# Expert units that leave y in PSUM over their end, loop conversions a step earlier, eight w_out tiles ahead

## The chip, the cores and the metric

The kernel runs on one core of a Trainium2 chip. The metric is the device time of one execution in microseconds (us), the median of several runs. Before the change it was 1417.6 us, the median of three runs from 1417.41 to 1417.85.

## The reference

All inputs but two are float32; `moe2_w_in` and `moe2_w_out` are float64.

```python
# attention: q, k, v are (8, 8, 576, 64); keys and values are averaged in blocks of 8
k_p, v_p = k.reshape(B, H, 72, 8, D).mean(3), v.reshape(B, H, 72, 8, D).mean(3)
scores = q @ k_p.T / sqrt(D)
attn = exp(scores - max); attn /= attn.sum(-1) + 1e-9
x = (attn @ v_p) as (4608, 512)
# first MoE: each of 4608 tokens goes to one of 8 experts (512 -> 1024 -> 512)
logits = x @ w_gate + modality_bias[modality_id]
e = argmax(logits); gate = softmax(logits)[e]
x = gate * (relu(x @ w1[e]) @ w2[e])
# second part, all tokens (512 -> 2048 -> 512)
h = x @ w_in
out = (h * clip(h + 3, 0, 6) / 6) @ w_out
```

## The kernel before

Float32 products are made of three matmuls of the type fp32r: each operand is split into a part hi, rounded to that type, and a rest lo, and hi·hi, hi·lo and lo·hi are summed in PSUM. A split costs a copy on ACT (hi, L771) and a subtraction on DVE (lo, L772).

The program has three stages. **Attention** and routing (to some 200 us) scatter the tokens to DRAM (`xr`), sorted by expert. The **units** (`moe1`, from some 197 to 648 us) each take 400 rows of one expert; this input makes twelve. Unit 0 is written out (`first`), eight run in a hardware loop (`For_i`, L1030), two follow in fixed code (`fs=0`, `fs=1`) and one is `last`. **`moe2`** (648 us to the end) computes the dense layers in 6 blocks of 768 tokens by 8 quads each; a quad has seven products `mm` (Strassen's scheme in Winograd's form) and twelve groups `o_group` of the product with `w_out`, which the next quad runs among its own `mm`.

A unit has eight steps f = 0..7, one for each 128 of the 1024 hidden columns. In step f, `h_mm(f)` makes 12 matmuls into a `ph` bank, ACT and DVE make hi and lo of its relu (L926, L927), and `y_mm(f - 1)` adds 12 matmuls into the four banks y0 to y3 (L935). `w_dma` loads the weights three steps ahead into two buffers `ws` (L865, L867), and `w_split` splits them two steps ahead on ACT and DVE. The next unit's rows (`cxg`) are loaded in steps 1 to 4, multiplied by their gate on POOL, and transposed on TensorE at the unit's end: `transp(c)` makes four transposes (L856; for c = 0 a fifth, L858, for the token numbers), and `split` takes them out of one of two `pt` banks as `xhi`, `xlo`. So `transp(2)` needs the bank of `transp(0)`, whose last reader is the copy `tkr` on ACT (L861), and `transp(3)` that of `transp(1)`, whose last reader is DVE's `xlo`.

At a unit's end PE runs `h_mm(7)`, `transp(0)`, `transp(1)`, `y_mm(6)`, `transp(2)`, `transp(3)`, `y_mm(7)`; then DVE copies y0 and y2 to `yo`, and ACT y1 and y3 (L1024), and `store_y` sends `yo` to DRAM in step 3 of the next unit.

While it runs, each unit of the loop also converts two pieces of the float64 `w_in` into the seven combinations that the quads use (`conv`, 13 operations each: 2 on ACT, 11 on DVE, loaded by L889, stored by L909). The fixed units and the first quads convert tiles of `w_out` (`wo_conv`, 9 operations each: 2 on ACT, 7 on DVE). `EARLY` names the tiles that are converted before `moe2`, `REST` those in its first block, where the list `cops` holds the operations and `extra[i]` places them behind product i of a quad.

PE, ACT, DVE and SP run what the program writes, in that order; an engine that waits holds back all that is behind it. All loads and most stores are issued by SP, so a store whose data are not ready also holds back the loads behind it. The loop's end is a branch on each engine; when the loop is left, all engines meet at a barrier.

Of the kernel before, what the change touches and what calls it, by code (L numbers as in the profile page):

```python
# [8 lines left out]
F32 = mybir.dt.float32  # L9
# [10 lines left out]
P = 128  # L20
# [9 lines left out]
NW = 400  # L30
# [8 lines left out]
YB = 8  # L39
NP = NT // (2 * TB)  # L40
NQ = F2 // (2 * P)
EARLY = (0, 8, 1, 9, 2, 10)
REST = (3, 11, 4, 12, 5, 13, 6, 14, 7, 15)
ORDER = (0, 4, 1, 5, 3, 2, 6)
KR = (0, 160, 288, 448)
GROUPS = ((0, 5), (5, 5), (10, 5), (15, 5), (20, 5), (25, 5), (30, 3), (33, 2), (35, 1))
# [752 lines left out]
def moe1(tc, g, xr_d, tok_d, y_d, s_d, w1, w2, w_in):  # L799
# [4 lines left out]
    def pool(n, b, st=es_l, **kw):  # L804
        return st.enter_context(tc.tile_pool(name=n, bufs=b, reuse_waits="tile", **kw))
# [18 lines left out]
    def open_ps():  # L824
        s.psy = pool("psy", 1, es_p, space=PSUM)
        s.psh = pool("psh", 2, es_p, space=PSUM)
        s.pst = pool("pst", 2, es_p, space=PSUM)

    def open3():
        g.open_w()  # L830
# [49 lines left out]
        gate_x()  # L880
        return i_

    def store_y(col):
        return nc.sync.dma_start(y_d.rearrange("(d p) n -> p d n", p=P)[:, :, bass.ds(col, NW)], s.yo)

    def conv_load(c, h, half):
        t = s.cs[h]
# [22 lines left out]

    def unit(i, first=False, last=False, tail=None, quad=None, fs=None):
        e = s.e0 if first else reg(0, i, E - 1)
        yps = [s.psy.tile([P, NW], F32, name=f"y{d}", tag=f"y{d}") for d in range(4)]
        hh = {}

        def h_mm(f):
            j = f % 4
            n = 0
            ph = s.psh.tile([P, NW], F32, name="ph", tag="ph")
            for k in range(4):  # L920
                for a, b in ((s.wh, s.xhi), (s.wh, s.xlo), (s.wl, s.xhi)):
                    nc.tensor.matmul(ph, a[j][:, 0, k * P:(k + 1) * P], b[k], start=(n == 0), stop=(n == 11))  # L922
                    n += 1
            hi = s.hp.tile([P, NW], F32R, name="hi", tag="hi")
            lo = s.hp.tile([P, NW], F32R, name="lo", tag="lo")
            nc.scalar.activation(hi, ph, AF.Relu)  # L926
            nc.vector.scalar_tensor_tensor(lo, ph, 0.0, hi.bitcast(F32), op0=ALU.max, op1=ALU.subtract)  # L927
            hh[f] = (hi, lo)

        def y_mm(f):  # L930
            j = f % 4
            hi, lo = hh.pop(f)
            for d in range(4):
                for n, (a, b) in enumerate(((s.wh, hi), (s.wl, hi), (s.wh, lo))):
                    nc.tensor.matmul(yps[d], a[j][:, 1, d * P:(d + 1) * P], b, start=(f == 0 and n == 0), stop=(f == 7 and n == 2))  # L935

        lx = LX if first else 1
        parts = {LX: (0, 1, 2, 3)} if first else {1: (0,), 2: (1,), 3: (2,), 4: (3,)}
        ops = []
        for f in range(8):  # L940
            if first and f == 0:
                w_dma(e, 2)
            if f == lx and not last:
                en = reg(0, i + 1, E - 1)
            if f < 5 or not last:
                w_dma(e if f < 5 else en, (f + 3) % 8)
            if f == 0 and not first:
                col = reg(5, i, NT)
                if quad is not None:
                    cc, cn = (nc.values_load(g.tab[0:1, 6, bass.ds(quad + d, 1)], engines=(ET.SP,), min_val=0, max_val=NQ - 1) for d in range(2))  # L950
            if f < 6 or not last:
                w_split((f + 2) % 8)
            h_mm(f)
            if f in parts and not last:
                load_x(i + 1, parts[f])
            if f - 1 in parts and not last:
                gate_x(parts[f - 1])
            if f == 2:
                store_tok(NT if first else reg(5, i + 1, NT))
            if f == 3 and not first:  # L960
                store_y(col)
            if f == 7 and not last:
                for c in range(2):
                    transp(c, ps())
            if f > 0:
                y_mm(f - 1)
            if tail and next(tail, None):
                open3()
            if first and f in (5, 6):
                conv_load(0, 0, f - 5)  # L970
            if first and f in (6, 7):
                g.wo_load(EARLY[f - 6])
            if first and f == 6:
                s.n_l = nc.values_load(g.nun, min_val=NQ, max_val=NQ + 8)
            if last:
                if f in (1, 2):
                    g.y_load(0, f - 1)
                if f == 3:
                    ops = g.y_ops(0)
                if f == 3:  # L980
                    nc.sync.dma_start(g.tk, tok_d[NW:NW + NT].rearrange("(c p) -> c p", p=P))
                if f == 7:
                    pt = ps()
                    nc.tensor.transpose(pt[:, 0:NT // P], g.tk, g.idn[0:NT // P, 0:NT // P])
                    nc.vector.tensor_copy(g.tki, pt[:, 0:NT // P])
                if f >= 1:
                    g.s_load()
                if f >= 3:
                    for _ in range(3):
                        if ops:  # L990
                            ops.pop(0)()
                if f >= 6:
                    g.wo_load(REST[f - 6])
            elif quad is not None:
                if f == 1:
                    co, ops = conv(s.cs[0])
                if f == 4:
                    c1_, ops = conv(s.cs[1])
                for _ in range(5):
                    if ops:  # L1000
                        ops.pop(0)()
                if f == 4:
                    conv_store(co, cc, 0)
                if f in (0, 1):
                    conv_load(cc, 1, f)
                if f in (5, 6):
                    conv_load(cn, 0, f - 5)
                if f == 7:
                    conv_store(c1_, cc, 1)
            elif fs is not None:  # L1010
                if f in (0, 2, 4):
                    ops += g.wo_conv(EARLY[3 * fs + f // 2])
                for _ in range(4):
                    if ops:
                        ops.pop(0)()
                n = 3 * fs + f // 2 + 1
                if f in (2, 4, 6) and n < len(EARLY):
                    g.wo_load(EARLY[n])
        if not last:
            for c in range(2, 4):  # L1020
                transp(c, ps())
        y_mm(7)
        for d in range(4):
            (nc.scalar.copy if d % 2 else nc.vector.tensor_copy)(s.yo[:, d], yps[d])  # L1024

    def run(tail):
        open_ps()
# [18 lines left out]
def moe2(tc, g, out):  # L1046
# [131 lines left out]
    yo = []  # L1178
    for j in range(NP):
        for q in range(NQ):  # L1180
            extra = {i: [] for i in range(7)}
            if j == 0:
                for i in range(7):
                    for _ in range(2):
                        if cops:
                            extra[i].append(cops.pop(0))
            if j + 1 < NP:
# [136 lines left out]
```

## Time and profile before

| | |
|---|---|
| median of 3 runs | 1417.6 us |
| profiled execution, its own time | 1416.87 us |
| its span, first to last instruction | 1415.1 us |
| granted TensorE clock, mean | 0.992 of full speed |
| busy: PE, DVE, ACT, POOL | 97%, 67%, 44%, 11% |

The profiled execution is 0.7 us faster than the median, and its time is 1.8 us longer than its span. Busy time of PE is no measure of its rate, since its matmuls overlap: one is shown with 340 ns and more, and the next one starts some 180 ns after it. What a wait costs is read from the distance of the starts. In a timeline, the bracket behind an instruction is the idle time before it and what ended it. The stage of the units is read at places where PE's order is the same in all units: their ends.

### The profile page before, as it was taken

The page shows a single profiled execution, that of the slowest core. Times are in us where ns is not written, and L with a number is a line of the kernel's source. Part 1 is how long each engine was busy: PE and PEld are TensorE (multiplying, and loading weights), DVE is VectorE, ACT ScalarE, POOL GpSimd, SP SyncE. Part 2 cuts the span into 40 slices and gives each one's busy share as a digit, 9 for nine tenths or more (in the row PEclk, how much of TensorE's full clock was granted, in tenths as well). Part 3 has the DMA queues.
Part 4 walks back from the last instruction along what each step waited for, and adds up shares of the span by engine and source line. Part 5 has one row for each costly group of instructions (what it writes and reads, how often), then busy time and mean ns, then how long its engine had stood idle before and what let it go on. Part 6 is the DMA issues. An engine that isn't in the chain of part 4 may idle for free.

```text
span 1415.1 us, 24118 instructions
## 1 busy us (share of the span) xinstructions
PE 1368.4 (97%) x7594; PEld 1263.5 (89%) x7594; DVE 947.2 (67%) x1929; ACT 627.6 (44%) x1276; POOL 159.3 (11%) x191
## 2 busy tenths in 40 slices
PE   7998989999999999999999999999999999999997
PEld 5888878999999999998888889888988888888886
DVE  6999785788888887876777445645644564465443
ACT  3576664555555554553444333423432343243322
POOL 3132331111111111100000100100010010001001
PEclk8899999999999999999999999999999999999999
DMA  9996356777777776675653544554354455345441
GB/s 254 314 273 203 108 167 197 245 245 246 246 244 243 243 241 199 188 223 169 202 163 114 184 142 120 159 162 119 120 181 140 120 150 173 116 119 164 115 116 67
DMA packets 229781, 254.40 MB, mean 180 GB/s; under 512 B 19256, under 2 KB 191836, under 8 KB 229692
## 3 DMA queue, kind: packets, MB, share of 16 engines
q1 hardware_dynamic: 223932, 233.16, 54.7%
q0 software_dynamic: 5760, 20.10, 4.0%
q8 instruction: 50, 0.82, 0.3%
q14 instruction: 39, 0.32, 0.1%
HBM read 206.74 MB, written 46.47 MB: 179 GB/s over the span
## 4 chain that ended last, share of the span: by engine, by line
issue 56%; PE 3%; POOL 2%; DVE 1%; ACT 0%; POOLq 0%; DVEq 0%; ACTq 0%
POOL out_dram L1074 2%; PE ph L922 2%; PE y L935 1%; DVE wl L772 0%; DVE wo L795 0%; DVE lo L927 0%; PE pt L856 0%; POOLq L1319 0%; ACT wh L771 0%; ACT dex L780 0%; DVE dex L794 0%; DVE dm L785 0%; DVE da L783 0%; ACT hi L926 0%; POOLq L1074 0%
## 5 line engine op out<-in xcount | busy, mean ns | idle before, releaser
L1095 PE MATMUL hps<-yc,sq 128*128 128x384 f32 x2004 | 405.2, 337 | 3.0 <-ACT s L1136 1.2
L1095 PEld LDWEIGHTS hps<-yc,sq 128*128 128x128 f32 x2004 | 358.2, 188 | 37.1 <-ACT s L1136 5.4
L1085 PE MATMUL ops<-wo,gh 128*128 128x512 f32 x1152 | 358.4, 392 | 0.0
L1085 PEld LDWEIGHTS ops<-wo,gh 128*128 128x128 f32 x1152 | 211.4, 188 | 23.1
L1085 PE MATMUL ops<-wo,gl 128*128 128x512 f32 x576 | 228.7, 397 | 0.0
L1107 ACT ACTIVATE r<-c,three 128x384 f32<-128x384 f32 x144 | 88.9, 617 | 207.8 <-DVE c L1117 205.8
L772 DVE TENSOR_TENSOR wl<-ws,wh 128x512 fp32r<-128x512 f32 x192 | 137.8, 751 | 33.4 <-ACT wh L771 29.3
L1111 ACT CAST gh<-r 128x384 fp32r<-128x384 f32 x192 | 98.6, 514 | 129.5 <-DVE r L1108 128.1
L771 ACT CAST wh<-ws 128x512 fp32r<-128x512 f32 x192 | 114.4, 619 | 76.0 <-DMA ws<-in_moe_w_dram 58.2
L922 PE MATMUL ph<-xhi,wh 128*128 128x400 f32 x384 | 132.3, 345 | 3.5 <-issue 1.3
L935 PE MATMUL y<-hi,wh 128*128 128x400 f32 x384 | 134.0, 349 | 0.1
L935 PE MATMUL y<-lo,wh 128*128 128x400 f32 x384 | 132.5, 345 | 1.3 <-DVE lo L927 1.3
L922 PE MATMUL ph<-xlo,wh 128*128 128x400 f32 x384 | 132.7, 346 | 0.2 <-DVE xlo L772 0.2
L922 PE MATMUL ph<-xhi,wl 128*128 128x400 f32 x384 | 132.7, 345 | 0.0
L935 PE MATMUL y<-hi,wl 128*128 128x400 f32 x384 | 131.4, 342 | 0.0
L1085 PEld LDWEIGHTS ops<-wo,gl 128*128 128x128 f32 x576 | 107.9, 187 | 23.1
L1112 DVE TENSOR_TENSOR gl<-r,gh 128x384 fp32r<-128x384 f32 x192 | 106.4, 554 | 27.5 <-ACT gh L1111 23.2
L1074 POOL DMA_INDIRECT out_dram<-osb,tki x36 | 35.3, 981 | 775.3 <-ACT osb L1072 743.5
L1108 DVE SCALAR_TENSOR_TENSOR r<-r,c 128x384 f32<-128x384 f32 x144 | 80.3, 558 | 55.3 <-ACT r L1107 53.4
L848 POOL TENSOR_TENSOR cxg<-cxg 100x512 f32<-100x512 f32 x48 | 57.7, 1205 | 343.8 <-PE ph L922 214.8
L1108 DVE SCALAR_TENSOR_TENSOR r<-r,hps 128x384 f32<-128x384 f32 x48 | 26.6, 553 | 97.6 <-ACT r L1107 96.1
L1107 ACT ACTIVATE r<-hps,three 128x384 f32<-128x384 f32 x48 | 27.9, 581 | 131.7 <-PE hps L1095 129.2
(220 smaller groups left out, 1908.1 us busy)
## 6 DMA issues: line engine op xcount, KB each, us to landing
sq<-sd SPq DMA_DIRECT2D x336, 256.0 KB
ws<-in_moe_w_dram SPq DMA_DIRECT2D x192, 256.0 KB, 3.8
sd<-wq SPq DMA_DIRECT2D x16, 896.0 KB, 4.1
cxg<-xr SPq DMA_DIRECT2D x44, 225.8 KB
yd<-yo SPq DMA_DIRECT2D x12, 800.0 KB, 5.7
yr<-yd SPq DMA_DIRECT2D x12, 768.0 KB
cs<-in_moe_w_in_dram SPq DMA_DIRECT2D x34, 256.0 KB, 3.8
kv<-in_k_dram SPq DMA_DIRECT2D x16, 512.0 KB
```

The source lines that it names most:

```text
L771: nc.scalar.copy(hi, src)
L772: nc.vector.tensor_tensor(lo, src, hi.bitcast(F32), op=ALU.subtract)
L848: nc.gpsimd.tensor_tensor(s.xg[:, t, 0:DM].rearrange("p (h x) -> p h x", x=D), v, s.xg[:, t, GC:GC + 1].unsqueeze(2).to_broadcast([T4, H, ...
L922: nc.tensor.matmul(ph, a[j][:, 0, k * P:(k + 1) * P], b[k], start=(n == 0), stop=(n == 11))
L935: nc.tensor.matmul(yps[d], a[j][:, 1, d * P:(d + 1) * P], b, start=(f == 0 and n == 0), stop=(f == 7 and n == 2))
L1074: i_ = nc.gpsimd.indirect_dma_start(out=out, out_offset=bass.IndirectOffsetOnAxis(ap=tki[:, c:c + 1], axis=0), in_=o, in_offset=None).ins
L1085: nc.tensor.matmul(pso[t_], gt[a][:, t * P:(t + 1) * P], wo[f][:, b], start=(q == 0 and fh == th and n == 0), stop=(q == NQ - 1 and fh != ...
L1095: nc.tensor.matmul(ps, w[:, kk, a * P:(a + 1) * P], y[:, b, kk], start=(start and n == 0), stop=(n == 5), skip_group_check=True)
L1107: a_.activation(r, c, AF.Relu, bias=g.three)
L1108: v.scalar_tensor_tensor(r, r, 6.0, c, op0=ALU.min, op1=ALU.mult)
L1111: a_.copy(gh, r)
L1112: late.append(lambda: v.tensor_tensor(gl, r, gh.bitcast(F32), op=ALU.subtract))
```

## The change

Five things are changed. The y banks are allocated once, and a unit (other than the first) begins with the copies of the y of the unit before (`y_out`); the last unit also copies its own at its end. At a unit's end, `y_mm(7)` is cut into y0 and y1, y2, and y3, and `transp(2)` and `transp(3)` stand between these. In the loop, the conversions of `w_in` begin in step 0 instead of 1 and end in step 5 instead of 6, and the second one's store is issued in step 6 instead of 7, ahead of that step 7's weight load. `yo` is stored in step 2 in the loop, in two halves in steps 3 and 5 of the fixed units, and in step 3 as before in the last one. `EARLY` has eight tiles instead of six: the last unit converts two more, the first quad converts none, and quads 1 to 6 convert the others, three operations behind their first product and two behind each of the next five.

```diff
--- before.py
+++ after.py
@@ -39,8 +39,8 @@
 YB = 8
 NP = NT // (2 * TB)
 NQ = F2 // (2 * P)
-EARLY = (0, 8, 1, 9, 2, 10)
-REST = (3, 11, 4, 12, 5, 13, 6, 14, 7, 15)
+EARLY = (0, 8, 1, 9, 2, 10, 3, 11)
+REST = (4, 12, 5, 13, 6, 14, 7, 15)
 ORDER = (0, 4, 1, 5, 3, 2, 6)
 KR = (0, 160, 288, 448)
 GROUPS = ((0, 5), (5, 5), (10, 5), (15, 5), (20, 5), (25, 5), (30, 3), (33, 2), (35, 1))
@@ -825,6 +825,7 @@
         s.psy = pool("psy", 1, es_p, space=PSUM)
         s.psh = pool("psh", 2, es_p, space=PSUM)
         s.pst = pool("pst", 2, es_p, space=PSUM)
+        s.y = [s.psy.tile([P, NW], F32, name=f"y{d}") for d in range(4)]
 
     def open3():
         g.open_w()
@@ -880,8 +881,12 @@
         gate_x()
         return i_
 
-    def store_y(col):
-        return nc.sync.dma_start(y_d.rearrange("(d p) n -> p d n", p=P)[:, :, bass.ds(col, NW)], s.yo)
+    def y_out():
+        for d in range(4):
+            (nc.scalar.copy if d % 2 else nc.vector.tensor_copy)(s.yo[:, d], s.y[d])
+
+    def store_y(col, a=0, b=4):
+        nc.sync.dma_start(y_d.rearrange("(d p) n -> p d n", p=P)[:, a:b, bass.ds(col, NW)], s.yo[:, a:b])
 
     def conv_load(c, h, half):
         t = s.cs[h]
@@ -910,8 +915,10 @@
 
     def unit(i, first=False, last=False, tail=None, quad=None, fs=None):
         e = s.e0 if first else reg(0, i, E - 1)
-        yps = [s.psy.tile([P, NW], F32, name=f"y{d}", tag=f"y{d}") for d in range(4)]
+        yps = s.y
         hh = {}
+        if not first:
+            y_out()
 
         def h_mm(f):
             j = f % 4
@@ -927,10 +934,10 @@
             nc.vector.scalar_tensor_tensor(lo, ph, 0.0, hi.bitcast(F32), op0=ALU.max, op1=ALU.subtract)
             hh[f] = (hi, lo)
 
-        def y_mm(f):
+        def y_mm(f, ds=range(4)):
             j = f % 4
-            hi, lo = hh.pop(f)
-            for d in range(4):
+            hi, lo = hh[f]
+            for d in ds:
                 for n, (a, b) in enumerate(((s.wh, hi), (s.wl, hi), (s.wh, lo))):
                     nc.tensor.matmul(yps[d], a[j][:, 1, d * P:(d + 1) * P], b, start=(f == 0 and n == 0), stop=(f == 7 and n == 2))
 
@@ -957,7 +964,9 @@
                 gate_x(parts[f - 1])
             if f == 2:
                 store_tok(NT if first else reg(5, i + 1, NT))
-            if f == 3 and not first:
+            if fs is not None and f in (3, 5):
+                store_y(col, f - 3, f - 1)
+            elif fs is None and not first and f == (3 if last else 2):
                 store_y(col)
             if f == 7 and not last:
                 for c in range(2):
@@ -975,8 +984,10 @@
             if last:
                 if f in (1, 2):
                     g.y_load(0, f - 1)
+                if f in (0, 2):
+                    ops += g.wo_conv(EARLY[6 + f // 2])
                 if f == 3:
-                    ops = g.y_ops(0)
+                    yo = g.y_ops(0)
                 if f == 3:
                     nc.sync.dma_start(g.tk, tok_d[NW:NW + NT].rearrange("(c p) -> c p", p=P))
                 if f == 7:
@@ -985,27 +996,29 @@
                     nc.vector.tensor_copy(g.tki, pt[:, 0:NT // P])
                 if f >= 1:
                     g.s_load()
+                for _ in range((4, 4, 4, 1, 1, 0, 1, 3)[f]):
+                    ops.pop(0)()
                 if f >= 3:
                     for _ in range(3):
-                        if ops:
-                            ops.pop(0)()
+                        if yo:
+                            yo.pop(0)()
                 if f >= 6:
                     g.wo_load(REST[f - 6])
             elif quad is not None:
-                if f == 1:
+                if f == 0:
                     co, ops = conv(s.cs[0])
-                if f == 4:
-                    c1_, ops = conv(s.cs[1])
-                for _ in range(5):
-                    if ops:
-                        ops.pop(0)()
+                if f == 3:
+                    c1_, o_ = conv(s.cs[1])
+                    ops += o_
+                for _ in range((3, 5, 5, 4, 5, 4, 0, 0)[f]):
+                    ops.pop(0)()
                 if f == 4:
                     conv_store(co, cc, 0)
                 if f in (0, 1):
                     conv_load(cc, 1, f)
                 if f in (5, 6):
                     conv_load(cn, 0, f - 5)
-                if f == 7:
+                if f == 6:
                     conv_store(c1_, cc, 1)
             elif fs is not None:
                 if f in (0, 2, 4):
@@ -1016,12 +1029,15 @@
                 n = 3 * fs + f // 2 + 1
                 if f in (2, 4, 6) and n < len(EARLY):
                     g.wo_load(EARLY[n])
+        y_mm(7, (0, 1))
         if not last:
-            for c in range(2, 4):
-                transp(c, ps())
-        y_mm(7)
-        for d in range(4):
-            (nc.scalar.copy if d % 2 else nc.vector.tensor_copy)(s.yo[:, d], yps[d])
+            transp(2, ps())
+        y_mm(7, (2,))
+        if not last:
+            transp(3, ps())
+        y_mm(7, (3,))
+        if last:
+            y_out()
 
     def run(tail):
         open_ps()
@@ -1179,9 +1195,9 @@
     for j in range(NP):
         for q in range(NQ):
             extra = {i: [] for i in range(7)}
-            if j == 0:
-                for i in range(7):
-                    for _ in range(2):
+            if j == 0 and q:
+                for i in range(6):
+                    for _ in range(3 if i == 0 else 2):
                         if cops:
                             extra[i].append(cops.pop(0))
             if j + 1 < NP:
```

The order on PE at the end of a unit of the loop, from the last matmul of `y_mm(6)` (operand hi_3641) to the first of `y_mm(7)` (hi_3680); `pt<-idn,cxg` are the transposes, `x4` four alike, REGISTER_ALU is the loop's address arithmetic. Before:

```order
L935 MATMUL y3_3293<-lo_3642,wh2_2521 128x400
L856 REGISTER_ALU
L856 MATMUL pt_3713<-idn_66,cxg_2047 128x100 x4
L856 REGISTER_ALU
L856 MATMUL pt_3720<-idn_66,cxg_2047 128x100 x4
L935 MATMUL y0_3290<-hi_3680,wh3_2522 128x400
```

Now, from the middle of `y_mm(7)`'s y0 on (its operands are hi_3677 and lo_3678), with `y_mm(6)` just ahead:

```order
L942 MATMUL y0_2767<-lo_3678,wh3_2522 128x400
L942 MATMUL y1_2768<-hi_3677,wh3_2522 128x400
L942 MATMUL y1_2768<-hi_3677,wl3_2526 128x400
L942 MATMUL y1_2768<-lo_3678,wh3_2522 128x400
L857 REGISTER_ALU
L857 MATMUL pt_3715<-idn_66,cxg_2047 128x100 x4
L942 MATMUL y2_2769<-hi_3677,wh3_2522 128x400
L942 MATMUL y2_2769<-hi_3677,wl3_2526 128x400
L942 MATMUL y2_2769<-lo_3678,wh3_2522 128x400
L857 REGISTER_ALU
L857 MATMUL pt_3725<-idn_66,cxg_2047 128x100 x4
L942 MATMUL y3_2770<-hi_3677,wh3_2522 128x400
```

Six matmuls of `y_mm(7)` now stand ahead of `transp(2)`, and nine ahead of `transp(3)`; before, both stood ahead of all twelve.

The order on DVE in the last steps of the loop's unit. `wx` and `wq` are the conversion (L897 and L905 before, L902 and L910 now), `wl` is the weights' lo, `lo` that of the hidden columns. Before, steps 6 and 7:

```order
L897 TENSOR_TENSOR wx<-wx 128x128
L905 REGISTER_ALU
L905 TENSOR_TENSOR wq<-wx,wq 128x7x128
L772 ISA
L772 TENSOR_TENSOR wl_2524<-ws_2058,wh_2520 128x512
L772 ISA
L772 TENSOR_TENSOR wl_2524<-ws_2058,wh_2520 128x512
L927 REGISTER_ALU
L927 SCALAR_TENSOR_TENSOR lo<-ph,hi 128x400
```

Now, from the end of step 5 to the first half of step 7's `wl`:

```order
L910 REGISTER_ALU
L910 TENSOR_TENSOR wq<-wx,wq 128x7x128
L772 ISA
L772 TENSOR_TENSOR wl_2523<-ws_2057,wh_2519 128x512
L772 ISA
L772 TENSOR_TENSOR wl_2523<-ws_2057,wh_2519 128x512
L934 REGISTER_ALU
L934 SCALAR_TENSOR_TENSOR lo<-ph,hi 128x400
L772 ISA
L772 TENSOR_TENSOR wl_2524<-ws_2058,wh_2520 128x512
L772 ISA
L772 TENSOR_TENSOR wl_2524<-ws_2058,wh_2520 128x512
```

The last operation of the conversion stood one `wl` pair and one `lo` ahead of the transposes' `xlo`; now there are two pairs of `wl` and two `lo` between them.

The order on DVE at the start of `moe2`, from the last copies of y on. `dm`, `da`, `dex`, `wo` belong to a conversion of `w_out`; `vv`, `ww`, `c`, `r`, `gl` to the first quad. Before:

```order
L1024 COPY yo<-y_4652 128x400
L1024 COPY yo<-y_4654 128x400
L781 TENSOR_SCALAR dm<-dex 128x512
L1117 TENSOR_TENSOR vv<-s_5051,hps 128x384
L782 TENSOR_SCALAR dm<-dm 128x512
L783 SCALAR_TENSOR_TENSOR da<-ds,sgn,dm 128x512
L1108 SCALAR_TENSOR_TENSOR r<-r,hps 128x384
L784 TENSOR_SCALAR dex<-da 128x512
L785 SCALAR_TENSOR_TENSOR dm<-ds,dex 128x512
L1117 TENSOR_TENSOR ww<-s_5051,hps 128x384
L1112 TENSOR_TENSOR gl<-r,gh 128x384
```

Now:

```order
L886 COPY yo<-y_2767 128x400
L886 COPY yo<-y_2769 128x400
L1133 TENSOR_TENSOR vv<-s_5065,hps 128x384
L1124 SCALAR_TENSOR_TENSOR r<-r,hps 128x384
L1133 TENSOR_TENSOR ww<-s_5065,hps 128x384
L1128 TENSOR_TENSOR gl<-r,gh 128x384
L1133 TENSOR_TENSOR c<-ww,ops_5105 128x384
L1124 SCALAR_TENSOR_TENSOR r<-r,c 128x384
L1133 TENSOR_TENSOR c<-s_5065,hps 128x384
L1128 TENSOR_TENSOR gl<-r,gh 128x384
```

The conversion's operations among those of the first quad are gone; they begin behind its last `gl`.

## Rows read from the trace of the kernel before

**Rows 1.** The page, part 1: busy time, share of the span and instructions of each engine.

```profile
PE 1368.4 (97%) x7594; PEld 1263.5 (89%) x7594; DVE 947.2 (67%) x1929; ACT 627.6 (44%) x1276; POOL 159.3 (11%) x191
```

**Rows 2.** PE's waits: who <- for whom: us in total, times, longest us.

```profile
PE pt L856 <- ACT tkr L861: 2.7, 3, 1.2
PE pt L856 <- DVE xlo L772: 1.6, 4, 0.5
PE y L935 <- DVE lo L927: 1.3, 3, 0.6
...
PE ph L922 <- PEq L1319: 1.2, 1, 1.2
...
PE hps L1095 <- ACT s L1136: 1.2, 2, 1.0
```

**Rows 3.** Timeline of PE, a unit's end without a wait: start us, us, what.

```profile
531.60 0.35 PE L935 MATMUL y<-lo,wh 128*128 128x400 f32 x1
531.79 0.85 PE L856 MATMUL pt<-idn,cxg 100*128 100x100 f32 x8
532.42 0.43 PE L935 MATMUL y<-hi,wh 128*128 128x400 f32 x1
```

**Rows 4.** Timeline of PE, end of the loop's first unit.

```profile
273.50 0.34 PE L935 MATMUL y<-lo,wh 128*128 128x400 f32 x1
275.08 0.56 PE L856 MATMUL pt<-idn,cxg 100*128 100x100 f32 x4 [1.23 <-ACT tkr L861]
276.11 0.56 PE L856 MATMUL pt<-idn,cxg 100*128 100x100 f32 x4 [0.47 <-DVE xlo L772]
276.45 0.43 PE L935 MATMUL y<-hi,wh 128*128 128x400 f32 x1
```

**Rows 5.** Timeline of PE, ends of unit 0 and of the second fixed unit.

```profile
234.86 0.35 PE L935 MATMUL y<-lo,wh 128*128 128x400 f32 x1
...
237.50 0.43 PE L935 MATMUL y<-hi,wh 128*128 128x400 f32 x1
...
608.32 0.34 PE L935 MATMUL y<-lo,wh 128*128 128x400 f32 x1
...
610.49 0.43 PE L935 MATMUL y<-hi,wh 128*128 128x400 f32 x1
```

**Rows 6.** Timeline of DVE, end of the loop's first unit.

```profile
271.45 1.09 DVE L905 TENSOR_TENSOR wq<-wx,wq 128x896 fp32r<-128x896 f32 x1 [1.01 <-ACT wq L904]
...
273.67 0.57 DVE L927 SCALAR_TENSOR_TENSOR lo<-ph,hi 128x400 fp32r<-128x400 f32 x1
...
277.31 0.57 DVE L772 TENSOR_TENSOR xlo<-pt,xhi 128x400 fp32r<-128x400 f32 x1 [0.46 <-ACT xhi L771]
```

**Rows 7.** Timeline of PE, the first two quads of moe2.

```profile
648.76 3.97 PE L1095 MATMUL hps<-yc,sq 128*128 128x384 f32 x20
652.57 1.21 PE L1095 MATMUL ops<-yc,sq 128*128 128x384 f32 x6
654.51 1.34 PE L1095 MATMUL hps<-yc,sq 128*128 128x384 f32 x6 [0.73 <-DVE ww L1117]
656.04 1.14 PE L1095 MATMUL ops<-yc,sq 128*128 128x384 f32 x5 [0.19 <-DVE c L1117]
...
663.17 1.14 PE L1095 MATMUL hps<-yc,sq 128*128 128x384 f32 x5 [0.96 <-ACT s L1136]
```

**Rows 8.** DMA issues in 325 to 327 us: issues, KB each, median us to landing.

```profile
ws<-in_moe_w_dram SPq DMA_DIRECT2D x2, 256.0 KB, 3.2
```

**Rows 9.** DMA issues in 334 to 336 us, just behind a store `sd` of 896 KB.

```profile
ws<-in_moe_w_dram SPq DMA_DIRECT2D x2, 256.0 KB, 6.5
```

**Rows 10.** Timelines of SP and ACT around a unit's end in the loop.

```profile
345.60 0.40 SPq L909 DMA_DIRECT2D sd<-wq  x1
...
352.59 0.62 ACT L771 CAST wh<-ws 128x512 fp32r<-128x512 f32 x1
```

**Rows 11.** Timeline of ACT at the loop's exit, the last copy of y.

```profile
534.92 0.49 ACT L1024 COPY yo<-y 128x400 f32<-128x400 f32 x1 [0.59 <-PE y L935]
```

## The prediction

> **What bounds the kernel now.** I read the page's busy times first. TensorE (PE) is busy for 97% of the span [rows 1] and no other engine for more than 67%, so the end moves only if PE waits less or does less. The change removes no matmul. What it can win is the time in which PE stands still in the units and in the first quads; behind these `moe2` runs on without a gap that the change touches. PE's own waits come next [rows 2]: in the units the largest are those of the transposes `pt`, 2.7 us for the copy `tkr` and 1.6 us for `xlo`, seven waits in all. Last come PE's timelines at the places where these fall, since the idle column shows less than a wait costs: what counts is the distance of the starts.
>
> The clean end of a unit is the measure [rows 3]: from the last matmul of `y_mm(6)` to the first of `y_mm(7)`, with eight transposes between, takes 532.42 - 531.60 = 0.82 us. The same stretch takes 276.45 - 273.50 = 2.95 us at the end of the loop's first unit [rows 4], 2.64 at the end of unit 0 and 2.17 at the end of the second fixed unit [rows 5]. The excess is 2.13, 1.82 and 1.35 us, 5.3 together. Of the four `xlo` waits, three belong to these ends (0.47 at one [rows 4], and the same cause at the other two); I put the fourth, at a later unit of the loop, at 0.3. So all unit ends together lose **5.6 us** to transposes that wait for a `pt` bank.
>
> At the start of `moe2` six matmuls of a product take (1.21 - 0.34)/5 = 0.174 us each [rows 7]. Measured against that, the 20 before 652.57 lose 0.33 us, the six from there 1.94 - 1.04 = 0.90, the six from 654.51 1.53 - 1.04 = 0.49. The wait for `s` at 663.17 shows 0.96; with the 0.17 by which the distance of starts exceeds the idle time in rows 4 (1.58 - 0.18 against 1.23) it costs 1.1. Sum: **2.8 us**, in a quad in which DVE does a conversion's operations between the sums that PE waits for.
>
> **The change, part by part.**
>
> *Transposes between the pieces of `y_mm(7)`.* Six matmuls, 6 x 0.18 = 1.1 us, now cover the copy `tkr`; nine and the first group of transposes, some 2.0 us, cover `xlo`. The waits to be covered are, at worst, 1.58 - 0.18 = 1.4 and 1.03 - 0.34 = 0.7 us [rows 4]. That leaves 0.3 us of the first, which the next part removes. In return `y_mm(7)` comes right behind `y_mm(6)` and needs its `lo` at once: in rows 4 the third matmul would start at 273.50 + 3 x 0.18 = 274.04, and DVE's `lo` ends at 273.67 + 0.57 = 274.24 [rows 6]. So here too 0.2 us would be left if DVE were as late as before. The price of splitting the transposes in two groups is not in the trace. Its bounds: nothing, as PE's starts follow on, or one slow start per group (the first matmul behind one shows 0.43 us, the one ahead 0.35 [rows 3]), 11 x 0.08 = 0.9 us. I take 0.4, the middle, as rows 3 show only one group of eight.
>
> *Conversions from step 0 to step 5.* None is added. At the end of the loop's first unit the last one on DVE, 1.09 us at 271.45 after 1.01 us of standing for ACT [rows 6], lies just ahead of `wl` and `lo`. It now lies a step (24 matmuls, 24 x 0.18 = 4.4 us) earlier, so `lo`, `xlo` and `tkr` come up to 2 us earlier, which covers the 0.3 and 0.2 us left above. With this the 5.6 us go in full. What hides the moved work in step 0 is that DVE there has only the y copies, one pair of `wl` and one `lo`. If that cover is gone, `lo` is late in the steps 1 to 5 instead (third rival).
>
> *The second store `sd` ahead of step 7's weight load.* SP runs in order, so the load now stands behind the store, and behind SP's wait for the conversion. A load right behind such a store lands in 6.5 us [rows 9], another in 3.2 [rows 8]: 3.3 us later, in each of eight passes. The old store was issued at 345.60 [rows 10]; the new one comes a step earlier, at 341.2, or up to 2 us later than that if DVE keeps some of its lag, and the load lands by 343.2 + 0.4 + 6.5 = 350.1 us. ACT splits it at 352.59 [rows 10]. So I put this at nothing: 2.5 us are left. The Trainium skill ("DMA: Bandwidth & Descriptors", Queues, rings and completion order) says that each DMA engine consumes the descriptors of a ring in order; by that the load waits for the whole store in every pass, the rows agree (6.5 against 3.2 us), and the sum stays unless the lateness outgrows the slack (second rival).
>
> *y left in PSUM, `y_out` in the next unit.* On ACT and DVE the copies stand between the same neighbours as before, `xlo` or `xhi` ahead and `wh`, `wl` behind; only the loop's branch has moved past them. No wait goes with this inside the loop. At the loop's exit all engines meet, and PE waits 1.2 us [rows 2]. The last to arrive was ACT's copy of y3, at 534.92 + 0.49 = 535.41 [rows 11]. Now it is DVE's `xlo` of `transp(3)`: in rows 4 and 6 it ends 277.88 - 276.11 = 1.77 us after the first of its transposes, which now starts some 0.72 us before the last matmul, so about 1.05 us after that one's start, where the copy ended 0.93 us after it. Nothing won, 0.1 lost; I take nothing. The store of `yo` moves by a step or is halved; no engine waits for it, and its buffer is next written a unit later. Nothing.
>
> *Eight `EARLY` tiles.* The first quad loses its conversion, and 2.8 us go. The last unit gains 18 operations, in steps 0 to 2 at the density of the fixed units (four a step); PE's only loss there at that density was a wait for `lo`, one of three with 1.3 us together [rows 2]. Bounds 0 to 0.8; I take 0, as the last unit has no gating on POOL beside it and two splits fewer. Quads 1 to 6 have 13 conversion operations in place of 14; their small waits I leave as they are.
>
> **Sum**: 5.6 + 2.8 - 0.4 = 8.0 us. The profiled execution took 1416.87 us (span 1415.1), which makes 1408.9; the median is 0.7 us above it, so I forecast **1409.6 us**.
>
> **Rivals.**
>
> *DVE and ACT are late for another cause, the weight loads.* The waits shrink only by what the matmuls cover. Then 0.5 us stay in the loop (the 0.3 and 0.2 above), unit 0 and the fixed unit, whose conversions are not moved, keep as much each, and in the second quad the copy `s` still stands behind the relu of the quad before, 1.1 us; with the price of splitting at its upper bound 0.9, the gain is 8.0 - 1.5 - 1.1 - 0.5 = 4.9, **1412.7 us**. For it: `s` is the last in its queue in any case. Against it: the idle 1.01 us of DVE beside the conversion [rows 6].
>
> *Slower: the load behind the store.* If SP stands a step (4.4 us) longer for the conversion, the load lands at 354.5 us instead of 350.1, `wh` and `wl` of step 2 follow 1.9 us later than in rows 10, and with them on the same queues hi and lo of step 0; PE then waits in each pass, and SP passes the lateness on to the next load. The price per pass is at least a `lo` wait (1.3/3 = 0.4) and at most the worst unit end (2.1); I take 1.5: 8 x 1.5 = 12, **1421.6 us**. It decides from 1.0 us a pass on. Against it: 2.5 us of slack ahead of the split, and PE wants hi and lo of step 0 only behind `h_mm(1)`, 24 x 0.18 = 4.4 us into the unit.
>
> *No change: the waits move to the steps.* Conversions from step 0 on make `lo` late once in a pass, at 0.9 us (the longest such wait, 0.6 [rows 2], with the 0.17 of distance and a slow start): 7.2 us of eight, **1416.8 us**. Against it: before, the same 26 operations in six steps cost the loop next to nothing.
>
> *More: also the waits for `lo`* (1.3 and 3 x 0.17 unseen) and the price of splitting (0.4) go: **1407.4 us**.
>
> **How the numbers follow.** Forecast 0.58, first rival 0.18, slower 0.08, no change 0.10, more 0.06. About 0.2% (2.8 us) is what a measurement can tell from no change; the forecast, the first and the last rival lie beyond it: faster 0.82, same 0.10, slower 0.08. The range from 1406.5 to 1414.5 holds these three cases with their bounds (splitting 0 to 0.9, the last unit 0 to 0.8) and leaves out the others, 0.18.
>
> **What would show it.** Right: PE's waits list no `pt` wait or one under 0.5 us; ends of units take about 0.82 us for eight transposes beside the matmuls between them; the first quads have no wait for `ww` or `s`; the wait at the loop's exit stays near 1.2; the waits for `lo` stay. Wrong: new waits of `ph` or `y` for `wl` or `lo` in the loop, `wh` standing for the DMA of step 7's load, or a wait of the first `y` of a unit for a copy of y.

## The result, and the profile after

The changed kernel took **1405.5 us** (median of 6 runs, 1402.9 to 1407.8) beside 1417.5 for the kernel before: a ratio of 0.9914, 95% interval 0.9901 to 0.9927, or 12.0 us. The direction was as forecast, but 8.0 us had been, and the time lies 1.0 us below the range. The profiled execution took 1405.17 us (span 1403.4).

The page's part 1, with the columns of [rows 1]:

```profile
PE 1362.4 (97%) x7594; PEld 1261.5 (90%) x7594; DVE 943.5 (67%) x1929; ACT 623.7 (44%) x1276; POOL 157.1 (11%) x191
```

As many matmuls as before, and PE still the bound. PE's waits from the units on, with the columns of [rows 2]:

```profile
PE ph L929 <- issue: 1.9, 1, 1.9
...
PE ph L929 <- PEq L1335: 1.4, 1, 1.4
...
PE y L942 <- DVE lo L934: 0.8, 2, 0.6
```

No wait of a `pt` is left of seven with 4.3 us, and none of `hps` of four with 2.4 (for `s` 1.2, for `ww` and `c` 1.2). The waits for `lo` are 0.8 us for 1.3, but the two later profiles of the kernel before have 0.8 and 0.6 as well. PE's timeline at the end of the loop's first unit, the place of [rows 4]:

```profile
271.61 0.35 PE L942 MATMUL y<-lo,wh 128*128 128x400 f32 x1
271.79 0.51 PE L857 MATMUL pt<-idn,cxg 100*128 100x100 f32 x4
272.08 0.43 PE L942 MATMUL y<-hi,wh 128*128 128x400 f32 x1
272.35 0.34 PE L942 MATMUL y<-hi,wl 128*128 128x400 f32 x1
272.53 0.35 PE L942 MATMUL y<-lo,wh 128*128 128x400 f32 x1
272.72 0.51 PE L857 MATMUL pt<-idn,cxg 100*128 100x100 f32 x4
273.00 0.43 PE L942 MATMUL y<-hi,wh 128*128 128x400 f32 x1
273.27 0.34 PE L942 MATMUL y<-hi,wl 128*128 128x400 f32 x1
```

Nothing in brackets: PE does not wait. A group of four takes 272.35 - 271.61 = 0.74 us to the second matmul behind it, of which two plain steps are 0.37; so 0.37 a group and 0.74 for both. In the kernel before, behind the eight in one group of [rows 3], the second matmul is

```profile
532.68 0.34 PE L935 MATMUL y<-hi,wl 128*128 128x400 f32 x1
```

so the eight cost 532.68 - 531.60 - 0.37 = 0.71. Cutting the group in two costs 0.03 us an end by this; by the six later passes of the loop, 218.72 us with the cut and 218.60 without it where neither waits (table below), 0.02. For eleven ends that is 0.2 to 0.3 us. At the start of `moe2`, the place of [rows 7], the first 42 products of quad 0 run through:

```profile
640.73 4.33 PE L1111 MATMUL hps<-yc,sq 128*128 128x384 f32 x24
644.90 1.20 PE L1111 MATMUL ops<-yc,sq 128*128 128x384 f32 x6
645.94 1.21 PE L1111 MATMUL hps<-yc,sq 128*128 128x384 f32 x6
646.98 1.24 PE L1111 MATMUL ops<-yc,sq 128*128 128x384 f32 x6
648.06 1.21 PE L1111 MATMUL hps<-yc,sq 128*128 128x384 f32 x6
```

It takes 648.06 - 640.73 = 7.33 us, where it took 657.19 - 648.05 = 9.14 before. What the forecast had not counted lies two quads on, in quad 2. There the trace of before has, on PE:

```profile
677.18 1.33 PE L1095 MATMUL hps<-yc,sq 128*128 128x384 f32 x6 [0.49 <-DVE c L1117]
...
680.16 1.14 PE L1095 MATMUL hps<-yc,sq 128*128 128x384 f32 x5 [0.26 <-ACT s L1136]
```

and the list of waits of the changed kernel has none of PE from 640 to 765 us, its quads 0 to 7.

### The profile page after: what moved, and what is told of

It reads as the page before. It is cut to its first block, busy times and chain, and to the rows that moved or that the text cites. A ratio compares the mean times of both kernels' runs of the same rounds, so it can differ in the third digit from the quotient of the medians.

```text
span 1403.4 us, 24126 instructions
## 1 busy us (share of the span) xinstructions
PE 1362.4 (97%) x7594; PEld 1261.5 (90%) x7594; DVE 943.5 (67%) x1929; ACT 623.7 (44%) x1276; POOL 157.1 (11%) x191
## 4 chain that ended last, share of the span: by engine, by line
issue 55%; PE 4%; POOL 2%; POOLq 0%; ACT 0%; DVE 0%; DVEq 0%
PE ph L929 2%; POOL out_dram L1090 2%; PE y L942 2%; PE pt L857 0%; POOLq L1335 0%; ACT yo L886 0%; DVE wl L772 0%; ACT wh L771 0%; POOLq L1090 0%; PE pt L859 0%; DVEq L934 0%
## 5 line engine op out<-in xcount | busy, mean ns | idle before, releaser
L772 DVE TENSOR_TENSOR wl<-ws,wh 128x512 fp32r<-128x512 f32 x192 | 131.1, 720 | 14.0 <-ACT wh L771 13.7
```

The costliest lines, as they stand in the source:

```text
L772: nc.vector.tensor_tensor(lo, src, hi.bitcast(F32), op=ALU.subtract)
```

## The experiments

All times of stages below are PE's, from the first `ph` of a unit or the first product of a quad to the next such start; a "pass" is one unit of the loop, and "exit" its eighth pass and the first fixed unit together. The kernel before itself took 1410 to 1411 us in three sessions and 1417.5 to 1418.3 in the other two; the traces put that difference mainly ahead of unit 0 (4.9 to 6.0 us), in code that no kernel here touches. So a time is compared only with that of the kernel before run beside it, and a stage only from unit 0 on.

| kernel | us, before beside it | ratio, 95% | unit 0 | pass 1 | passes 2-7 | exit | 2nd fixed | quads 0-2 | quads 3-7 |
|---|---|---|---|---|---|---|---|---|---|
| before | 1417.5 | | 43.32 | 38.68 | 219.51 | 75.93 | 38.60 | 43.02 | 79.09 |
| before, again | 1410.0, 1410.5 | 0.9987-1.0008 | 41.39 | 40.02 | 219.69 | 76.23 | 37.69 | 43.01 | 79.09 |
| third profile of before | 1419.1, 1418.3 | one run | 44.25 | 38.53 | 219.12 | 77.39 | 37.74 | 43.02 | 79.10 |
| changed | 1405.5, 1417.5 | 0.9901-0.9927 | 41.54 | 36.90 | 218.72 | 76.61 | 36.47 | 38.70 | 78.86 |
| changed, again | 1398.2, 1410.5 | 0.9904-0.9930 | 40.36 | 36.93 | 218.72 | 75.97 | 36.47 | 38.67 | 78.88 |
| cut alone | 1404.2, 1410.2 | 0.9944-0.9969 | 40.27 | 36.58 | 218.72 | 76.98 | 37.06 | 43.01 | 79.02 |
| conversions alone | 1406.1, 1410.2 | 0.9966-0.9984 | 41.75 | 36.90 | 218.60 | 75.76 | 37.99 | 42.99 | 79.05 |
| eight tiles alone | 1405.5, 1410.2 | 0.9960-0.9982 | 41.43 | 38.39 | 219.83 | 75.88 | 38.18 | 38.70 | 79.02 |
| y alone | 1406.6, 1410.2 | 0.9965-0.9983 | 41.63 | 37.89 | 218.87 | 75.36 | 37.60 | 43.01 | 79.00 |
| no cut | 1401.7, 1410.5 | 0.9923-0.9949 | 41.09 | 36.61 | 218.61 | 75.65 | 38.36 | 38.67 | 78.88 |
| conversions late | 1405.5, 1418.3 | 0.9892-0.9920 | 40.71 | 37.02 | 218.72 | 75.96 | 36.47 | 38.70 | 78.88 |
| six tiles | 1402.0, 1410.5 | 0.9931-0.9957 | 39.90 | 36.54 | 218.72 | 75.96 | 36.44 | 43.00 | 79.04 |
| store twice | 1422.4, 1418.3 | 1.0021-1.0047 | 41.17 | 36.86 | 230.54 | 80.59 | 37.26 | 38.67 | 79.12 |
| two each | 1407.1, 1418.3 | 0.9904-0.9931 | 41.85 | 36.76 | 218.72 | 76.28 | 36.44 | 38.66 | 80.66 |
| quad 0 empty | 1409.9, 1411.2 | 0.9986-1.0016 | 43.46 | 39.80 | 220.38 | 75.92 | 37.26 | 38.66 | 82.09 |

**One part at a time, in the kernel before.** Each edit is the piece of the change's diff that belongs to the part. The cut:

> The kernel before with the cut of y_mm(7) alone. Theory A (the parts act where the prediction put them): the matmuls between cover the waits for a pt bank except 0.3 and 0.2 us in the loop's first unit, which belong to the late conversion; unit 0, the second fixed unit and the later unit of the loop are covered. Gain 5.6 - 0.5 = 5.1, so about 1412.4 us beside a before of 1417.5. Theory B (the transposes are late for the weight loads as well, and the second pt group just waits elsewhere): 0.5 us stay at each of three ends, gain 4.1, 1413.4. Theory C (the split of the transposes costs 0.4): one us half way between, told by the distance of the starts around pt in a clean unit: 0.82 us for both groups in A, over 1.0 in C. The attention stage's code is that of before: if the 1.5 us by which the changed kernel began unit 0 earlier was chance, this kernel's first product starts anywhere between 195 and 197 us; if it belongs to the change, within 0.3 us of 196.7.

6.0 us (ratio 0.9957). Pass 1 takes 36.6 us, as short as in any kernel, with no wait at its end: the 0.3 and 0.2 us that theory A left there are not left. The sign of theory C, over 1.0 us for both groups, is absent (0.02 to 0.03 above). The eighth pass takes 38.98 us, where both profiles of the changed kernel have 38.02: here the copies of y stand behind `xlo` of the late `transp(3)` and ahead of the barrier, where PE waited 2.35 us. The first product of unit 0 came at 189.6 us, outside both bounds set for it; see below.

> The kernel before with the loop's conversions in steps 0 to 5 and their second store in step 6, and nothing else. Theory A: lo, xlo and tkr of the loop's unit ends come up to 2 us earlier, which takes the whole wait there: 2.13 in the first pass and 0.3 to 0.7 in later ones, gain 2.4 to 2.8, about 1414.9 us; unit 0 and the second fixed unit keep 1.82 and 1.35. Theory B (late for the weight loads): nothing is won at the loop's end, 1417.5. Slower rival: a store ahead of step 7's load costs 1.0 us or more in each of eight passes, 1425; with A no pass shows a wait for wh or hi behind it.

4.1 us (0.9975). Pass 1 comes to 36.9 us and passes 2 to 7 to 218.6, unit 0 and the second fixed unit keep their waits: theory A of the cause. Against 38.6 us, pass 1 of the first and third profile of before, that is 1.7 us, and 0.8 in the later passes: 2.5, as expected. The other 1.6 of the 4.1 lie where this part does nothing. The store ahead of the load costs no pass anything.

> The kernel before with eight w_out tiles ahead and nothing else: the last unit converts two more, the first quad none, the quads 1 to 6 three operations behind the first product and two behind the next five. Theory A (as predicted): the first two quads win 2.8 us, and what quads 1 to 6 lost stays, 1414.7 us. Theory B (the waits of the quads 1 to 6 go too, since the operation on ACT and the one on DVE that waits for it no longer fall behind one product just ahead of the sum that PE wants): 2.8 and another 1.2 to 1.7, 4.0 to 4.5, about 1413.3 us, of which quad 0 wins 1.8, quad 1 1.2, quad 2 1.3. The last unit's 18 operations cost 0 in both.

4.7 us (0.9971). The quads 0 to 2 win 4.32 us, the quads 3 to 7 nothing, the last unit is as long as ever: theory B.

> The kernel before with y left in PSUM over a unit's end, its copies in the next unit and the stores that go with it. Theory A (as predicted): nothing, 1417.5 within 0.3. Theory B: the copies behind the loop's exit make it later: the changed kernel lost 0.2 us from the exit's barrier and 0.5 in the unit behind it; so 1418.2, with the wait of PE some ten matmuls behind the exit at 1.9 us in place of 1.3. Theory C: halving the stores of the fixed units takes the wait for lo in the second of these (0.69 us by starts), 1416.8; it decides whether the rest of that unit's gain over the forecast comes from the stores.

3.6 us (0.9974), which none of the three theories had. The stages are those of pass 1, the later passes and the exit. SP's first weight load of the loop and PE's first matmul of pass 1, in the second profile of the kernel before:

```profile
233.47 0.39 SPq L865 DMA_DIRECT2D ws<-in_moe_w_dram  x1
```

```profile
233.24 0.45 PE L922 MATMUL ph<-xhi,wh 128*128 128x400 f32 x1
```

and with y alone changed:

```profile
231.02 0.39 SPq L866 DMA_DIRECT2D ws<-in_moe_w_dram  x1
```

```profile
232.17 0.34 PE L929 MATMUL ph<-xhi,wh 128*128 128x400 f32 x1
```

The load went out 0.23 us behind the matmul and now goes out 1.15 ahead of it: the copies of unit 0's y no longer stand ahead of the loop's entry. SP's wait there was 4.4 us for ACT's branch, and is 2.7 for DVE's. All of pass 1's loads come 1.4 us earlier against PE, and its last conversion on DVE 0.6 to 0.8, which fits the 0.7 us that pass 1 is shorter. With the cut that is gone again (0.03 to 0.08 us behind, in both profiles of the changed kernel); in the changed kernel without the cut the load goes out 1.15 us ahead, as here. That `xlo` of `transp(3)` is what comes last there follows from the order, and is not shown. Of theory C, the 0.69 us of `lo` in the second fixed unit are absent in the second and third profile of the kernel before too: chance.

**The whole change, and without one part.** The four gains add up to 18.3 us, the whole gives 12.4 (1398.2 beside 1410.5). Cut, conversions and y each take the same waits at the end of pass 1: from 38.6 us they win 2.0, 1.7 and 0.7 alone and 1.7 together, which is 2.7 of the 5.9 too many. The rest is not settled; 1.6 of it are those of the conversions that no stage of theirs holds.

> The kernel before, unchanged. Each of the four parts alone came out 3.6 to 6.0 us faster than it, in sum 18.3 us, where the whole change gave 12.0: some 3 us seem to be common to all four. Theory A (a part of the time before the units is chance or belongs to the chip): in this profile the attention stage is as in the four, the first product of unit 0 at 189.6 to 190.6 us if the chip is that of those runs, and the granted clock of the first 60 us 0.83, 0.83, 1.00 as in theirs. Theory B (the kernel before has a loss of its own ahead of the units, which any of the parts takes away): the first product comes 1.5 us or more behind that of the changed kernel run beside it, with the clock at 0.91, 0.75, 0.91 as in the trace of before.

> The changed kernel, unchanged. Theory A: the ratio 0.9914 holds on every chip; 12 us below the before run beside it. Theory B: what came ahead of the units (1.5 us) does not come again, ratio 0.9925, 10.5 us. In both the stages behind the first product of unit 0 win 10.2 us, as in the first pair of traces: 1.8 at unit 0's end, 1.8 in the loop's first pass, 2.1 in the second fixed unit, 4.3 in the quads 0 to 3, 0.8 in the later passes, less 0.7 at the loop's exit.

The ratio holds, 0.9917. Ahead of unit 0 the two profiles differ by 1.7 us, as the first two did by 1.5, which is the sign of theory B. But the code there is unchanged, and it took from 189.6 to 192.3 us in the eight kernels of these two sessions, the longest in the changed kernel without the cut, run beside these. So chance is large enough for it; whether a little of it belongs to the change remains open.

> The changed kernel with transp(2) and transp(3) ahead of all of y_mm(7) again. Theory A: unit 0 and the second fixed unit lose 1.8 and 1.3 us again, the first fixed unit up to 0.8, the loop next to nothing since its conversions end earlier; so 3.1 to 4.0 us above the changed kernel beside it. Theory B (the cut alone makes the gain at the ends): the loop's first pass loses 2.1 as well, 5.6 in all.

3.6 us above the changed kernel, as theory A has it, but not for its reasons alone: by the profiles 2.2 us lie ahead of unit 0, in unchanged code, and the difference of the two ratios, 0.0019, has an uncertainty as large as itself. From unit 0 on 1.9 us are lost: 1.9 in the second fixed unit and 0.7 in unit 0, where PE waits for `tkr` again (1.3 us), less 0.3 each in pass 1 and at the exit. That pass 1 stays short puts theory B out; of theory A the size is not shown.

> The changed kernel with the loop's conversions in steps 1 to 6 and the second store in step 7 again. Theory A (the prediction's): the cut alone leaves 0.3 and 0.2 us at the end of the loop's first pass, and lo late now and then in later passes; 0.5 to 0.8 us above the changed kernel. Theory B (the cut alone was enough there: made alone, it brought the first pass to 36.6 us, as short as in the whole change): within 0.3 us of the changed kernel, first pass 36.5 to 36.9, passes 2 to 7 218.7 us. The exit from the loop may be 0.3 either way.

```diff
-                if f == 0:
+                if f == 1:
                     co, ops = conv(s.cs[0])
-                if f == 3:
+                if f == 4:
...
-                if f == 6:
+                if f == 7:
                     conv_store(c1_, cc, 1)
```

0.9906 against 0.9914: no loss that can be measured, theory B. Pass 1 takes 37.0 us for 36.9. Its last conversion on DVE begins 31.39 us into the pass, as late as before, and the third matmul of `y_mm(7)` comes 0.25 us late for its `lo`; no transpose waits. So the cut makes the earlier conversions all but needless.

> The changed kernel with six w_out tiles ahead and the first quads as before. Theory A (as predicted): 2.8 us above the changed kernel, all in the quads 0 and 1. Theory B: 4.0 to 4.5, quads 2 and 3 too, as when this part was made alone (no wait of a product for c or s in the quads 1 to 3 then, three with 2.2 us by starts without it).

3.8 us above the changed kernel; by stages 4.3 in the quads 0 to 2: theory B.

**The store ahead of the load.**

> The changed kernel with the second store of the loop's conversions issued twice, so that step 7's weight load stands behind 1792 KB; the output is the same. The loads behind one store landed 3.3 us later than others, so some 3.3 us more. Theory A (2.5 us of slack ahead of the split, as the prediction worked out, and 4.4 ahead of hi and lo): wh and wl of the unit's first split come 1 to 2 us late and PE loses 0 to 0.5 us a pass, 0 to 4 us in eight. Theory B (the slower rival): once the load outgrows the slack, its lateness goes on to the next loads, 1.5 us a pass or more, over 12 us.

```diff
                 if f == 6:
                     conv_store(c1_, cc, 1)
+                    conv_store(c1_, cc, 1)
```

The ratio goes from 0.9914 to 1.0034, 17 us. Passes 2 to 7 lose (230.54 - 218.72)/6 = 2.0 us each, the eighth and the first fixed unit together 4. Its lists of waits have, for PE and for SP from 270 to 540 us (us in total, times, longest):

```profile
PE y L942 <- DVE lo L934: 6.7, 17, 1.0
```

```profile
SPq L914 <- DMA sd<-wq: 28.7, 8, 3.9
```

The edit does something else than was expected of it. Both stores write the same place, and SP does not issue the second before the first has landed: 3.6 us in each pass. The load therefore stands behind one store, as in the changed kernel, and lands 5.2 us after its issue; but it is issued 4.1 us later. That is the slower rival's own condition, SP standing almost a step longer, and its price is 2.0 us a pass for the 1.5 it was given: theory B. The lateness is passed on: the store of the pass's first piece goes out 21.9 us into pass 2, and 18.0 in the changed kernel. What two stores ahead of a load cost where SP does not stand, no run shows.

**The first quads.**

> The changed kernel with two operations of a w_out conversion behind each of the seven products of the quads 1 to 5 (14 a quad), in place of three behind the first and two behind the next five. Both leave quad 0 empty. Theory A (the waits in the quads 1 and 2 went because quad 0 is empty and the list starts a quad later, whatever the pattern): the quads 1 and 2 stay at 15.7 us each, quad 3 at 16.1 or less. Theory B (the pattern did it: with 13 a quad the ACT operation and the DVE operations behind it fall at the same products in each quad, away from those whose c or s PE wants; with 14 they drift): some of the quads 1 to 5 lose 0.3 to 1.3 us, in sum 1 to 2.5 us above the changed kernel.

```diff
-                for i in range(6):
-                    for _ in range(3 if i == 0 else 2):
+                for i in range(7):
+                    for _ in range(2):
```

Both theories hold in part: the quads 0 to 2 stay at 38.7 us, but the quads 3 to 7 lose 1.8, at waits for `s` and `c`. By time it can't be told from the changed kernel (0.9917).

> The kernel before with six w_out tiles ahead as it has, but no conversion operation in quad 0: the list of the other ten begins in quad 1, two behind each product. Theory A (an empty quad 0 is enough: the conversion that starts there sets off the waits of the quads 1 and 2): quad 0 7.3, quads 1 and 2 15.7 us each, as with eight tiles ahead, so 4.3 us off these three. Theory B (the waits of quads 1 and 2 hang on where the list stands): quad 0 wins 1.8, and what quads 1 and 2 lost comes back a quad later, 1.2 to 2.4 us.

```diff
-            if j == 0:
+            if j == 0 and q:
                 for i in range(7):
```

Theory A for these three quads, 4.36 us. In quad 3 the conversions' operations stand as they stood in quad 2 before, and DVE waits for the same operation on ACT just ahead of the `c` that PE wants. Before, and with quad 0 empty:

```profile
675.97 0.69 DVE L794 TENSOR_TENSOR dex<-da,wo 128x512 f32<-128x512 f32 x1 [1.10 <-ACT wo L793]
```

```profile
680.49 0.69 DVE L794 TENSOR_TENSOR dex<-da,wo 128x512 f32<-128x512 f32 x1 [1.10 <-ACT wo L793]
```

The first is 1.9 us into its quad (from 674.08) and the second 1.1 (from 679.39), and the quads lose 1.3 and 0.5 us to the 15.69 of a clean one. So some 0.8 us of quad 2's loss had come in from the quads ahead, and 0.5 is due to the operations of the quad itself.

But the ten tiles now reach into the later quads, where PE's waits (quads 1 to 8) are

```profile
PE hps L1095 <- DVE c L1117: 1.3, 3, 0.6
PE hps L1095 <- ACT s L1136: 0.8, 2, 0.5
```

and the quads 3 to 7 lose 3.0 us, the rest 0.7. By time nothing is won (ratio 1.0001). An empty quad 0 takes the waits of quads 0 to 2 away; two tiles fewer and 13 operations a quad keep others from coming later (with two tiles fewer and 14 a quad, as above, 1.8 us came).

**A stretch at half the clock.**

> The kernel before, unchanged, one profile. In its second profile nine matmuls behind the wait at the end of the loop's first pass ran at a granted clock of 0.50, 0.33 us each in place of 0.18, which cost 1.4 us; in the first profile they did not. Theory A (it falls to half after a long stand of PE, now and then): the first pass takes 38.4 to 38.7 us without such a stretch or 39.8 to 40.0 with one. Theory B (a part of each program, not of the run): 40.0 again, as this is the program of the second profile.

Pass 1 took 38.5 us: theory A. But unit 0 has such a stretch in this profile (stretch, PE's busy time and count, granted clock, share of DMA, GB/s):

```profile
238.50:241.70 3.20, 3.20 (x11) 0.50 0.03 5
```

The second profile of the kernel before, PE's timeline behind the wait at the end of pass 1:

```profile
268.11 0.56 PE L856 MATMUL pt<-idn,cxg 100*128 100x100 f32 x4 [1.07 <-ACT tkr L861]
269.15 0.56 PE L856 MATMUL pt<-idn,cxg 100*128 100x100 f32 x4 [0.47 <-DVE xlo L772]
...
270.59 0.54 PE L935 MATMUL y<-hi,wl 128*128 128x400 f32 x1
270.92 0.54 PE L935 MATMUL y<-lo,wh 128*128 128x400 f32 x1
271.26 0.54 PE L935 MATMUL y<-hi,wh 128*128 128x400 f32 x1
```

and the stretches ahead, in it and behind:

```profile
264.00:266.80 2.80, 2.80 (x22) 1.00 0.51 155
270.26:273.25 2.99, 2.99 (x10) 0.50 0.47 135
273.50:275.00 1.50, 1.50 (x10) 1.00 0.41 133
```

Nine starts at 0.33 us in place of 0.18 cost 1.4 us, at the lower of the two levels (0.50 is 1.2 GHz). PE had stood 1.07 and 0.47 us just ahead. In the three profiles of the kernel before there are two such stretches at these ends, and the kernel with quad 0 empty has one at each; the two of the changed kernel have none there.

## Why the prediction was right in sign and short in size

The three profiles of the kernel before against the two of the changed one, by means: unit 0 2.0 us, pass 1 2.2, passes 2 to 7 0.7, exit 0.2, second fixed unit 1.5, quads 4.6, in sum 11.2. The interval of the ratio is 10.3 to 14.0 us, so this leaves nothing that must be explained. But in the first pair of profiles 1.5 of 11.7 us lie ahead of unit 0, where unchanged code varies by more. That the time fell beyond the range, by 1.0 us, may be chance; that the gain is larger than forecast is not, as the quads show in every profile.

- *"their small waits I leave as they are"* (quads 1 to 6) **failed**, and is the largest miss: I put the start of `moe2` at 2.8 us, and it gave 4.55. The quads 0 and 1 gave 3.0, as forecast; quad 2 gave 1.3 that I had put at nothing. Some 0.8 of it had come in from the quads ahead, with the conversion in quad 0, and 13 operations a quad with two tiles fewer kept the later quads nearly as they were (14 a quad: 1.8 us worse).
- *The price of splitting, 0.4* for eleven ends, was too high: 0.02 to 0.03 us an end, 0.2 to 0.3 in all, and inside its bounds.
- *Ends of units, 5.6*, held in its places: 1.82 forecast for unit 0 and 2.0 found, 2.13 and 2.2, 1.35 and 1.5; the later passes gave 0.7 for 0.3. A part of unit 0 and pass 1 was no wait but the half clock behind one: two stretches of 1.4 us in three profiles, 0.9 us in the mean. The first trace of before had none, so neither the sum nor the range held it. Unit 0 also varies by itself: over all kernels with the cut it took 39.9 to 41.9 us.
- *"With this the 5.6 us go in full"* gave the earlier conversions a part that they do not have: the cut alone clears pass 1, and without them the whole change loses 0.1 us there. The 0.2 us for `lo` were right where DVE is as late as before (0.25 with the conversions late); with the cut alone its last conversion began 30.95 us into the pass, for 31.41 and 31.25 in the first two profiles of before, and the 0.2 went. The 0.3 for `tkr` show in neither.
- *y left in PSUM: "Nothing"* was wrong for the part alone, since I looked at the loop's exit and not at its entry, and right in the whole change, where the cut takes the entry back. At the exit it is what keeps the cut from costing 1.0 us; there 0.1 lost was forecast, and PE's wait for the barrier went from 1.2 to 1.4 us.
- *"The waits for lo stay"* held: 0.8 us now, and 1.3, 0.8 and 0.6 in the three profiles of before, of which the 0.6 at the first step of unit 0 is in every kernel.
- *The slower rival*: where SP stood 3.6 us longer, the mechanism came and cost 2.0 us a pass for 1.5; that the change itself does not reach it was right. The first rival (`s` of the second quad late in any case) is refuted: that wait is gone in every kernel with an empty quad 0.

The range stopped at 1406.5 because the only case that I had beyond the forecast was the waits for `lo`; the small waits behind the part that was removed were a better one.

## What to carry to other kernels

Where a change takes work off an engine that is late, follow that engine's lateness past the last wait that the work touches itself: here a part of the waits two quads on went with it. A wait of PE near 2 us can cost more than it shows, since the clock may fall behind it (here nine matmuls at half speed, 1.4 us); and parts that take away the same wait do not add, so one of them may be needless. At a loop look at the entry as well as at the exit: what stands last ahead of it holds back the first loads.

## What was not expected of the hardware

After the loop PE stops once more, some ten matmuls behind the barrier: 1.9 and 1.3 us in the two profiles of the changed kernel, 1.3, 1.6 and 1.5 in those of before, 0 in the kernel with the conversions alone, and in the kernel with the cut alone none either, but nine matmuls at 0.33 us. In most profiles nothing is named that ended this stop; in four of kernels with the whole change or most of it, among them the second of the changed kernel, it is a `wl` on DVE. The cause is open. That the granted clock falls to 0.50 for some 3 us behind a stand is no rule: behind the two waits of [rows 4], 2.1 us by starts, it stayed at 1.00 (276.5 to 279.5 us), and so it did in the first profile of before at the exit, behind a wait of 1.2 us. And the kernel before, unchanged, took 1410 or 1418 us by the session, with the same matmul rate in the units; why the stage ahead of unit 0 was 5 to 6 us longer in the one is open.
